# Random-feature attention, a dense layer and a top-1 MoE: the planner gets a shared port and margins, 16 subtractions change from GpSimd to VectorE, the clearing of the output stands later

## The chip, the core and the metric

The kernel runs on one core of a Trainium2 chip. The core has five engines with a queue of instructions each: TensorE (PE, matrix products), VectorE (DVE), ScalarE (ACT), GpSimd (POOL) and SyncE (SP, which here only starts DMA transfers). SBUF and PSUM are the on-chip memories. The metric is the device time in microseconds; lower is better.

## What is computed

```python
# attention with random features; q, k, v: 2 x 8 heads x 576 x 64, omega: 128 x 64
def phi(x):
    h = einsum('bhsd,md->bhsm', x, omega) - sum(x * x, -1) / 2
    return exp(h - max(h, -1)) / sqrt(m)
q_p, k_p = phi(q * scale), phi(k * scale)
kv, z = einsum('bhsm,bhsd->bhmd', k_p, v), sum(k_p, axis=2)
x = einsum('bhsm,bhmd->bhsd', q_p, kv) / (einsum('bhsm,bhm->bhs', q_p, z) + 1e-6)
# dense layer: x 1152 x 512, w_in 512 x 2048, w_out 2048 x 512, both weights as 64-bit floats
h = x @ w_in
y = (h * clip(h + 3, 0, 6) / 6) @ w_out
# MoE: 8 experts, each token to the one with the largest of y @ w_gate, at most 288 tokens each
out[i] = gate[i] * (relu(y[i] @ w1[e]) @ w2[e])      # rows that find no place stay 0
```

## The kernel before

**Attention.** The rows of q and k come in 18 units of 128 x 512, in the order of the list `seq` (five units of k, then q and k alternating, then q). A unit goes through a chain. ScalarE rounds it to its upper half xh (L778); the lower half xl = x - xh is one subtraction of two SBUF tiles (L780), on GpSimd for units 2 to 17 (`X_POOL`), else on VectorE. Then for each of its two halves of 128 x 512 TensorE multiplies with omega (pj, L790), VectorE takes the maximum of each row (nm, L796: 36 of these in all), and ScalarE forms the exponentials (phi, L802), which read the PSUM bank of pj and set it free. Units of k are summed up with v (kvp, L817); those of q are transposed (tpC, L847, copied by ScalarE), multiplied (nd, L863), divided by VectorE (x, L885), transposed again (tpE, L891) and split into the two halves of xT by ScalarE (L914) and VectorE (L917).

**Unpacking the weights.** w_in and w_out come as 16 pieces each of 128 x 512 64-bit numbers, loaded by SyncE (L220, L222) into four buffers. `wlist` gives their order: four pieces of w_in, four of w_out, and so on, 32 in all (weights 0 to 31). Each is turned into 32-bit floats by a chain of five instructions: take the sign off (an AND on VectorE, L248, or, from weight `ABS_FROM` = 12 on, an Abs on ScalarE, L246), clamp (L250), shift (L252), join the lower word (L254), join sign and exponent (L256). A piece of w_in (tiles x, later wsplit) is then split like q and k: the upper half by ScalarE (L262), the lower half by a subtraction (L264, in the plan WL), on GpSimd for weights before `ABS_FROM`, so for eight pieces of w_in, else on VectorE. A piece of w_out (tiles wo) is transposed by TensorE (tpW, L299, in the plan T), copied by ScalarE (woT, L302) and, four at a time, multiplied with the gate's weights (wogp, L309).

**The dense layer.** For each of the 16 f-tiles and each of three groups of 384 tokens there is one block of twelve products hp (L277, 48 blocks); then ScalarE forms t = relu(h + 3) (L281), VectorE g (L285, in the plan Hg), and SyncE writes g to DRAM (L287, L290). The logits of the gate (lg, L334) gather g times the folded gate weights. Then come routing and the experts, which are the same in both kernels but for their place in the queues.

**What sets the order.** Every piece of work is a step of one `Plan`: engine, cost, the steps that it waits for, the buffers that it takes and frees, a rank. `Plan.order` simulates the engines with these costs, always takes the step that could begin first, the lowest rank among those that are ready, and so writes one queue per engine. Rank is a number per kind of step, plus the unit, plus a shift per kind from the table `DELTA`. The chip then runs each queue in just that order; costs and times in the plan have no other effect. A later instruction of a queue never overtakes an earlier one that waits.

The output must hold zeros where no token lands: GpSimd sets a blank tile to 0 (L379) and SyncE writes it nine times over the output (L380), 2304 KB. In the plan this is the step Lout, after `consts`, a string of small GpSimd steps.

Of the kernel before, what the change touches and what calls it, by code (L numbers as in the profile page):

```python
# [39 lines left out]
class Plan:  # L40
# [14 lines left out]
    def add(self, name, engine, cost, emit, after=(), takes=None, frees=(), rank=0.0, early=0.0, then=()):  # L55


        st = dict(
            name=name, engine=engine, cost=cost, emit=emit, after=list(after), frees=list(frees),
            takes=[(takes, name)] if isinstance(takes, str) else takes or [],  # L60
            rank=rank + self.shift, early=early, end=None, then=list(then), kind=self.kind(name),
        )
        self.steps.append(st)
        self.named[name] = st

    def order(self):
# [3 lines left out]
        free_at = {}  # L70
        waiting = {}
# [10 lines left out]
        def begin(st):  # L82
# [17 lines left out]
            return max(free_at[st["engine"]], st["early"], t + self.into.get(st["engine"], 0.0) if t else 0.0)  # L100

        out = []
        for _ in self.steps:
# [15 lines left out]
            free_at[st["engine"]] = st["end"]  # L119
            waiting[st["engine"]].remove(st)  # L120
# [11 lines left out]
def moe_kernel(ctx, tc, q, k, v, v_rest, omega, w_in, w_out, w_gate, w1, w2, out, cap):  # L132
# [31 lines left out]
    X_POOL = set(range(2, 18))  # L164
# [8 lines left out]
    ABS_FROM = 12  # L173
    SLACK = dict(DVE=0.14)
    DELTA = {'consts': 172.4, 'XH0': 7.9, 'XL0': 162.8, 'OM': 17.4, 'OL': -135.3, 'B0': -35.7, 'N0': -102.4, 'P0': 43.4, 'XH1': 5.0, 'XL1': -25.3, 'B1': -28.8, 'N1': -83.0, 'P1': 52.0, 'XH2': 412.1, 'XL2': -95.8, 'B2': -8.2, 'N2': 67.1, 'P2': -3.7, 'KT': 274.4, 'K0': -8.3, 'KW': 141.3, 'KV': -15.6, 'K1': 15.7, 'C1': 127.6, 'T1': 91.1, 'D1': 17.2, 'R1': 27.8, 'S1': -0.4, 'X1': 178.6, 'E1': 182.5, 'EH1': 45.1, 'EL1': -150.5, 'C2': -8.8, 'T2': 158.1, 'D2': 96.9, 'R2': 12.6, 'S2': 129.1, 'X2': 17.9, 'E2': -20.4, 'EH2': 146.6, 'EL2': -87.9, 'KR': -30.3}
# [53 lines left out]

    def w_fetch(key):  # L230
        loaded[key] = w_load(*key)

    def decode(key):
# [30 lines left out]
        (nc.vector if key in abs_act else nc.gpsimd).tensor_tensor(out=t[:, 1, :], in0=xf, in1=t[:, 0, :].bitcast(F32), op=ALU.subtract)  # L264
# [834 lines left out]
    for n, (kd, f) in enumerate(wlist):  # L1099
# [12 lines left out]
        if kd == "i":  # L1112
# [3 lines left out]
                (f"WL{nm}", *(("DVE", 0.6) if (kd, f) in abs_act else ("Pool", 1.25)), dict(after=[f"w{nm}"], frees=[f"W0{nm}"], rank=n if (kd, f) in abs_act else -300)),  # L1116
# [25 lines left out]
    for n, (_, f, g) in enumerate(order):  # L1142
# [5 lines left out]
            (f"Hg{me}", "DVE", 0.47, dict(after=[f"Ht{me}"], takes="g", frees=[f"H{me}", f"Ht{me}"], rank=-500 + n)),  # L1148
# [288 lines left out]
```

## Time and profile before

| | before |
|---|---|
| median of 3 runs | 331.89 us (331.43 to 333.74) |
| profiled execution | 332.73 us |
| its span (first to last instruction) | 330.9 us |
| TensorE clock granted, mean | 0.99 of full speed |
| busy: TensorE, VectorE, ScalarE, GpSimd | 306.9, 222.3, 177.5, 65.4 us |

The busy times are shares of the span of 93, 67, 54 and 20 per cent. Such a share is an average over stages with different limits, so the tables by stage matter more. In the rows further down, x is a tile's name, "x16" a count, and "A <- B" in a table of waits means that A stood until B was done.

### The profile page before, as it was taken

What the parts mean: (1) busy time and instruction counts of PE and PEld (TensorE: products, weight loads), DVE (VectorE), ACT (ScalarE), POOL (GpSimd) and SP (SyncE); (2) the same over time, 40 slices, a digit from 0 to 9 for tenths busy, and PEclk for the clock granted to TensorE, in tenths of its full rate; (3) what the DMA queues carried; (4) which work ended last, traced back from release to release, by engine and by line L of the source; (5) the groups of instructions that cost most, each with busy time, mean ns of one, the idle gap of its engine ahead of it and who ended that gap; (6) DMA issues with size and microseconds to landing.
All of it is one profiled execution on the core that took longest, in us unless ns stands there. A gap on an engine that the chain in (4) does not pass through costs nothing.

```text
span 330.9 us, 6974 instructions
## 1 busy us (share of the span) xinstructions
PE 306.9 (93%) x2570; PEld 278.7 (84%) x2570; DVE 222.3 (67%) x474; ACT 177.5 (54%) x427; POOL 65.4 (20%) x68
## 2 busy tenths in 40 slices
PE   8985989999997798999999999898999999999992
PEld 5884978999987596887989888698999989999781
DVE  5589899999999889889985354749955002764100
ACT  6988799984643545453766324533555132633110
POOL 0774813400240000000000000411513012511021
PEclk9998999999999999999999999999999999999998
DMA  7998662124458777877235127891770004710011
GB/s 245 362 317 309 248 231 66 64 90 137 138 176 254 263 226 234 271 229 223 97 127 184 49 74 244 280 318 57 235 255 1 2 24 101 274 50 0 4 48 32
DMA packets 29675, 54.10 MB, mean 163 GB/s; under 512 B 5536, under 2 KB 18208, under 8 KB 29632
## 3 DMA queue, kind: packets, MB, share of 16 engines
q1 hardware_dynamic: 29248, 52.38, 48.2%
q0 software_dynamic: 384, 1.18, 1.1%
q8 instruction: 22, 0.36, 0.5%
q14 instruction: 21, 0.17, 0.2%
HBM read 37.42 MB, written 16.13 MB: 162 GB/s over the span
## 4 chain that ended last, share of the span: by engine, by line
PE 51%; DVE 15%; DMA 15%; issue 9%; ACT 4%; POOL 2%; SPq 1%; POOLq 0%; ACTq 0%; DVEq 0%
PE hp L277 14%; PE yw L571 14%; PE hp L639 6%; DMA raw<-in_w_in_dram 4%; PE yq L661 4%; PE pj L790 4%; DMA raw<-in_w_out_dram 3%; PE nd L863 3%; DVE nm L796 2%; DMA rawe<-in_w_dram 2%; PE lg L334 2%; DMA out_dram<-scratch,to 2%; DVE g L285 2%; DMA rawx<-in_k_dram 2%; DVE x L252 2%
## 5 line engine op out<-in xcount | busy, mean ns | idle before, releaser
L277 PE MATMUL hp<-xT,wsplit 128*128 128x384 f32 x576 | 107.8, 340 | 0.0
L277 PEld LDWEIGHTS hp<-xT,wsplit 128*128 128x128 f32 x576 | 98.9, 188 | 5.1 <-issue 5.0
L618 POOL TENSOR_TENSOR wsplit<-rawe,wsplit 128x512 fp32r<-128x512 f32 x16 | 22.0, 1379 | 160.6 <-ACT wsplit L616 141.6
L571 PE MATMUL yw<-gh,ohi 128*128 128x288 f32 x256 | 51.9, 298 | 0.2 <-ACT scratch L701 0.2
L281 ACT ACTIVATE t<-hp,three 128x384 f32<-128x384 f32 x48 | 27.6, 578 | 31.4 <-PE hp L277 30.1
L802 ACT ACTIVATE phi<-pj,nm 128x128 f32<-128x128 f32 x144 | 41.0, 414 | 5.5 <-DVE nm L796 5.4
L571 PEld LDWEIGHTS yw<-gh,ohi 128*128 128x128 f32 x256 | 40.8, 188 | 1.3 <-issue 0.6
L285 DVE SCALAR_TENSOR_TENSOR g<-t,hp 128x384 f32<-128x384 f32 x48 | 26.4, 549 | 18.3 <-ACT t L281 17.5
L564 DVE TENSOR_TENSOR gh<-gw,gh 128x288 fp32r<-128x288 f32 x32 | 18.0, 578 | 30.1 <-ACT gh L562 27.8
L571 PE MATMUL yw<-gh,olo 128*128 128x288 f32 x128 | 37.6, 294 | 0.0
L790 PE MATMUL pj<-wbd,xh 128*128 128x256 f32 x144 | 26.3, 305 | 6.5 <-ACT phi L802 5.7
L796 DVE TENSOR_REDUCE nm<-pj 128x4 f32<-128x512 f32 x36 | 24.6, 684 | 5.5 <-ACT phi L802 3.6
L790 PEld LDWEIGHTS pj<-wbd,xh 128*128 128x128 f32 x144 | 19.7, 192 | 10.1 <-ACT phi L802 7.6
L780 POOL TENSOR_TENSOR xl<-rawx,xh 128x512 fp32r<-128x512 f32 x16 | 21.7, 1361 | 30.7 <-ACT xh L778 17.5
L562 ACT ACTIVATE gh<-gw 128x288 fp32r<-128x288 f32 x32 | 14.0, 442 | 23.7 <-PE yw L571 21.1
L639 PE MATMUL hp<-dT,wsplit 128*128 128x288 f32 x192 | 26.3, 296 | 0.4 <-DVE dT L583 0.4
L639 PEld LDWEIGHTS hp<-dT,wsplit 128*128 128x128 f32 x192 | 25.7, 188 | 0.6 <-DVE dT L583 0.6
L571 PEld LDWEIGHTS yw<-gh,olo 128*128 128x128 f32 x128 | 24.1, 189 | 0.0
L616 ACT ACTIVATE wsplit<-rawe 128x512 fp32r<-128x512 f32 x32 | 19.0, 622 | 1.3 <-DMA rawe<-in_w_dram 1.1
L264 POOL TENSOR_TENSOR wsplit<-x,wsplit 128x512 fp32r<-128x512 f32 x8 | 11.6, 1450 | 29.9 <-ACT wsplit L262 29.9
L689 PE MATMUL yp<-wsplit,h 128*96 128x512 f32 (+1 forms) x96 | 16.9, 337 | 0.0
L689 PEld LDWEIGHTS yp<-wsplit,h 128*96 128x96 f32 x96 | 13.5, 162 | 3.4
(147 smaller groups left out, 454.0 us busy)
## 6 DMA issues: line engine op xcount, KB each, us to landing
gall<-g SPq DMA_DIRECT2D x48, 192.0 KB, 3.1
raw<-in_w_in_dram SPq DMA_DIRECT2D x16, 512.0 KB, 4.8
raw<-in_w_out_dram SPq DMA_DIRECT2D x16, 512.0 KB, 4.7
rawe<-in_w_dram SPq DMA_DIRECT2D x16, 512.0 KB, 5.3
gfirst<-g SPq DMA_DIRECT2D x16, 192.0 KB, 3.7
rawx<-in_q_dram SPq DMA_DIRECT2D x9, 256.0 KB, 6.4
out_dram<-blank SPq DMA_DIRECT2D x1, 2304.0 KB, 9.3
gw<-gfirst SPq DMA_DIRECT2D x16, 144.0 KB, 2.6
```

The costliest lines, as they stand in the source:

```text
L277: nc.tensor.matmul(hp, lhsT=w[:, a, wk], rhs=xT[g][b_][:, kk, :], start=(n == 0), stop=(n == 3 * KD - 1))
L281: nc.scalar.activation(out=t, in_=hp, func=ACTF.Relu, bias=three[:, 0:1])
L285: nc.vector.scalar_tensor_tensor(out=gv, in0=t, scalar=6.0, in1=hp, op0=ALU.min, op1=ALU.mult)
L571: nc.tensor.matmul(self.ps[kk], lhsT=wohalf[f][a][:, kk * 128:(kk + 1) * 128], rhs=self.gh[f][:, b_, :], start=(f == YORDER[0] and n == 0) ...
L616: nc.scalar.activation(out=hi, in_=part, func=ACTF.Copy)
L618: engine.tensor_tensor(out=lo, in0=part, in1=hi.bitcast(F32), op=ALU.subtract)
L639: nc.tensor.matmul(hp, lhsT=self.w[0, f][:, a, kk * 128:(kk + 1) * 128], rhs=self.window.dT[b_][:, kk, :], start=(n == 0), stop=(n == 3 * ...
L689: nc.tensor.matmul(ps_, lhsT=self.h2[f // 4, a][:, f % 4, c * SR:(c + 1) * SR], rhs=self.w[1, f][:, b_, x * w:(x + 1) * w], start=(n == 0) ...
L780: (nc.gpsimd if u in X_POOL else nc.vector).tensor_tensor(out=lo[:, sl], in0=rawt[u][:, sl], in1=hi[:, sl].bitcast(F32), op=ALU.subtract)
L790: nc.tensor.matmul(pj[:, 2 * jj:2 * jj + 2, :], lhsT=a[:, j, :], rhs=w, start=(jj == 0 and n == 0), stop=(n == 2), skip_group_check=True,)
L796: nc.vector.tensor_reduce(out=nm, in_=pj, axis=AX.X, op=ALU.max, negate=True)
L802: nc.scalar.activation(out=phis[u][:, 4 * half + h, :], in_=pj[:, h, :], func=ACTF.Exp, bias=nm[:, h:h + 1])
```

## The change

Seven things change.

1. `X_POOL` becomes units 2 to 9: xl of units 10 to 17 is made by VectorE.
2. `POOL_TO = 0`: all lower halves of w_in (WL) are made by VectorE, also those of the first eight pieces.
3. `ABS_FROM` goes from 12 to 8: of weights 8 to 11 the sign is taken off by ScalarE.
4. The plan gets a resource `port`: steps of VectorE and GpSimd whose names match one of two patterns cannot overlap in the plan.
5. The plan gets `lag`: Hg is planned 1.0 us, T 1.5 us behind what they wait for.
6. Lout gets a rank of its own and is planned at 58 us at the earliest; it costs the plan 0.5 and not 6.6 us.
7. Planned costs of the loads are higher, and `DELTA` has new numbers.

The names in the code of steps: W0 to W4 are the five instructions of unpacking, WL the subtraction, XL the subtraction for q and k.

```diff
-            rank=rank + self.shift, early=early, end=None, then=list(then), kind=self.kind(name),
+            port=bool(re.match(r"(XL|WL|v)\d*" if engine == "Pool" else r"(W[0-9L]|XL|OL|ol|gl|v\d)", name)) and engine in ("DVE", "Pool"),
+            rank=rank + self.shift, early=early, lag=lag, end=None, then=list(then), kind=self.kind(name),
...
+        port = [0.0]
...
-            return max(free_at[st["engine"]], st["early"], t + self.into.get(st["engine"], 0.0) if t else 0.0)
+            return max(port[0] if st["port"] else 0.0, free_at[st["engine"]], st["early"], t + self.into.get(st["engine"], 0.0) + st["lag"] if t else 0.0)
...
             free_at[st["engine"]] = st["end"]
+            if st["port"]:
+                port[0] = st["end"]
...
-    X_POOL = set(range(2, 18))
+    X_POOL = set(range(2,10))
...
-    ABS_FROM = 12
+    ABS_FROM = 8
+    POOL_TO = 0
+    LAG_G, LAG_T = 1.0, 1.5
+    OUT_AT = 58.0
...
-    DELTA = {'consts': 172.4, 'XH0': 7.9, 'XL0': 162.8, 'OM': 17.4, 'OL': -135.3, 'B0': -35.7,
...
+    DELTA = {'consts': 116.2, 'XH0': 36.4, 'XL0': 424.6, 'OM': 132.2, 'OL': -14.2, 'B0': 118.9,
...
+    on_pool = set(wlist[:POOL_TO])
...
-        (nc.vector if key in abs_act else nc.gpsimd).tensor_tensor(out=t[:, 1, :], in0=xf, in1=t[:, 0, :].bitcast(F32), op=ALU.subtract)
+        (nc.gpsimd if key in on_pool else nc.vector).tensor_tensor(out=t[:, 1, :], in0=xf, in1=t[:, 0, :].bitcast(F32), op=ALU.subtract)
...
-        load(f"w{i}", lambda: w_fetch(wlist[i]), 1.46, "raww")
+        load(f"w{i}", lambda: w_fetch(wlist[i]), 1.65, "raww")
...
-    load("out", clear_out, 6.6)
-    plan.named["Lout"]["after"].append("consts")
+    plan.add("Lout", "SP", 0.5, clear_out, after=["consts"], rank=-960.0, early=OUT_AT)
...
-                (f"WL{nm}", *(("DVE", 0.6) if (kd, f) in abs_act else ("Pool", 1.25)), dict(after=[f"w{nm}"], frees=[f"W0{nm}"], rank=n if (kd, f) in abs_act else -300)),
+                (f"WL{nm}", *(("Pool", 1.25) if (kd, f) in on_pool else ("DVE", 0.6)), dict(after=[f"w{nm}"], frees=[f"W0{nm}"], rank=-300 if (kd, f) in on_pool else n)),
...
-            (f"Hg{me}", "DVE", 0.47, dict(after=[f"Ht{me}"], takes="g", frees=[f"H{me}", f"Ht{me}"], rank=-500 + n)),
+            (f"Hg{me}", "DVE", 0.47, dict(lag=LAG_G if f < F1T - TAIL else 0.0, after=[f"Ht{me}"], takes="g", frees=[f"H{me}", f"Ht{me}"], rank=-500 + n)),
...
-                (f"T{f}o", "PE", 0.44, dict(after=[f"W4o{f}"] + attended, takes="tp", frees=[f"W0o{f}"], rank=NG * (f - BLOCK) + 0.6)),
+                (f"T{f}o", "PE", 0.44, dict(lag=LAG_T, after=[f"W4o{f}"] + attended, takes="tp", frees=[f"W0o{f}"], rank=NG * (f - BLOCK) + 0.6)),
```

The other loads' costs change likewise (0.73 to 0.83, 1.48 to 1.7). Line numbers of the changed kernel are 8 higher at the loads of the weights (L220 is L228) and 10 higher from there on (L248 is L258).

How the queues look at three places follows; a row has the line, the operation, output tile <- input tiles, and the shape. Names carry a number each, so that rows of one tile can be told.

**VectorE among the row maxima (nm).** The queue from its 17th instruction on, first of the kernel before; x32 is a piece of w_in that is being unpacked:

```order
L248 TENSOR_SCALAR x32_426<-raw_356 128x512
L250 TENSOR_SCALAR x32_426<-x32_426 128x512
L796 TENSOR_REDUCE nm_452<-pj_419 128x4
L252 TENSOR_SCALAR x32_426<-x32_426 128x512
L254 SCALAR_TENSOR_TENSOR x32_426<-raw_356,x32_426 128x512
L256 SCALAR_TENSOR_TENSOR x32_426<-raw_356,x32_426 128x512
L796 TENSOR_REDUCE nm_481<-pj_462 128x4
L248 TENSOR_SCALAR x32_500<-raw_469 128x512
L250 TENSOR_SCALAR x32_500<-x32_500 128x512
L796 TENSOR_REDUCE nm_519<-pj_502 128x4
L252 TENSOR_SCALAR x32_500<-x32_500 128x512
L796 TENSOR_REDUCE nm_541<-pj_522 128x4
```

and of the changed kernel:

```order
L806 TENSOR_REDUCE nm_432<-pj_418 128x4
L258 TENSOR_SCALAR x32_452<-raw_412 128x512
L260 TENSOR_SCALAR x32_452<-x32_452 128x512
L806 TENSOR_REDUCE nm_478<-pj_459 128x4
L806 TENSOR_REDUCE nm_504<-pj_490 128x4
L262 TENSOR_SCALAR x32_452<-x32_452 128x512
L850 TENSOR_TENSOR kvz_530<-kvp_234,kvrs_500 128x8x65
L806 TENSOR_REDUCE nm_543<-pj_519 128x4
L852 TENSOR_TENSOR kvz_530<-kvz_530,kvp_234 128x8
L264 SCALAR_TENSOR_TENSOR x32_452<-raw_412,x32_452 128x512
L806 TENSOR_REDUCE nm_567<-pj_552 128x4
L266 SCALAR_TENSOR_TENSOR x32_452<-raw_412,x32_452 128x512
```

Before, eight unpacking instructions stand among four maxima there; in the changed kernel five stand among five maxima, with two sums of kvz.

**ScalarE where the first transposes of w_out are copied (woT).** Before (t is the ReLU of a hidden block, wsplit the upper half of a piece of w_in, and L246 the Abs of a piece of w_out):

```order
L281 ACTIVATE t_1504<-hp_1472,three_82 128x384
L914 ACTIVATE xT02_98<-tpE_1498 128x2x256
L914 ACTIVATE xT02_98<-tpE_1506 128x2x256
L281 ACTIVATE t_1561<-hp_1513,three_82 128x384
L302 ACTIVATE woT_1569<-tpW_1556 128x512
L302 ACTIVATE woT_1578<-tpW_1563 128x512
L302 ACTIVATE woT_1587<-tpW_1571 128x512
L302 ACTIVATE woT_1603<-tpW_1580 128x512
L262 ACTIVATE wsplit_1608<-x32_1495 128x512
L281 ACTIVATE t_1631<-hp_1589,three_82 128x384
L262 ACTIVATE wsplit_1635<-x32_1585 128x512
L246 ACTIVATE wo_1652<-raw_1605 128x512
```

and of the changed kernel, where L256 is the Abs:

```order
L291 ACTIVATE t_1542<-hp_1485,three_82 128x384
L256 ACTIVATE x32_1546<-raw_1501 128x512
L291 ACTIVATE t_1557<-hp_1529,three_82 128x384
L312 ACTIVATE woT_1574<-tpW_1552 128x512
L291 ACTIVATE t_1588<-hp_1561,three_82 128x384
L312 ACTIVATE woT_1605<-tpW_1583 128x512
L256 ACTIVATE x32_1610<-raw_1577 128x512
L291 ACTIVATE t_1631<-hp_1591,three_82 128x384
L291 ACTIVATE t_1644<-hp_1618,three_82 128x384
L256 ACTIVATE x32_1660<-raw_1615 128x512
L312 ACTIVATE woT_1665<-tpW_1639 128x512
L272 ACTIVATE wsplit_1670<-x32_1546 128x512
```

Before, the first four transposes follow one another behind the first block or two; in the changed kernel they stand one by one between hidden blocks and Abs instructions.

**SyncE around the clearing of the output.** Before (rawx is a unit of q or k, raw a piece of weight, out_0 the output):

```order
L728 DMA rawx_593<-in_q_dram 128x512
L222 DMA raw_600<-in_w_out_dram 128x512
L222 DMA raw_638<-in_w_out_dram 128x512
L380 DMA out_0_dram<-blank_677 128x9x512
L728 DMA rawx_813<-in_q_dram 128x512
L728 DMA rawx_823<-in_q_dram 128x512
L222 DMA raw_839<-in_w_out_dram 128x512
L222 DMA raw_861<-in_w_out_dram 128x512
```

and of the changed kernel, where L390 is the clearing and gall1 and gfirst1 are the first writes of g:

```order
L738 DMA rawx_633<-in_q_dram 128x512
L230 DMA raw_648<-in_w_out_dram 128x512
L738 DMA rawx_681<-in_q_dram 128x512
L738 DMA rawx_744<-in_q_dram 128x512
L230 DMA raw_859<-in_w_out_dram 128x512
L390 DMA out_0_dram<-blank_1146 128x9x512
L230 DMA raw_1152<-in_w_out_dram 128x512
L297 DMA gall1_101<-g_1206 128x384
L300 DMA gfirst1_117<-g_1206 128x384
L230 DMA raw_1353<-in_w_out_dram 128x512
```

Before, the clearing stands ahead of the loads of the last two units of q; in the changed kernel it stands behind them. Six loads of weights stand ahead of it in both, four of them before the first row shown here.

## Rows read from the trace of the kernel before

**Rows 1.** Stages: us, busy time (x instructions) per engine, PEclk, DMA share, GB/s

```profile
16.00:36.00 20.00, 15.60 (x199) 13.82 (x195) 17.22 (x31) 16.92 (x55) 12.60 (x23) 0.91 0.77 270
36.00:54.00 18.00, 16.65 (x222) 15.00 (x220) 17.69 (x37) 15.79 (x49) 7.66 (x6) 1.00 0.71 247
54.00:69.00 15.00, 14.92 (x216) 14.11 (x215) 14.63 (x41) 15.00 (x49) 5.13 (x4) 1.00 0.12 38
...
83.00:101.00 18.00, 16.36 (x128) 14.35 (x127) 17.52 (x28) 9.09 (x18) 5.66 (x4) 1.00 0.54 172
101.00:150.00 49.00, 44.05 (x317) 39.03 (x320) 42.86 (x84) 26.86 (x51) 0.00 (x0) 1.00 0.79 245
150.00:190.00 40.00, 40.00 (x269) 35.12 (x264) 28.72 (x58) 21.07 (x42) 0.00 (x0) 1.00 0.38 133
```

**Rows 2.** Waits, 16 to 75 us: who <- releaser: total us, times, longest

```profile
POOL xl L780 <- ACT xh L778: 9.6, 6, 2.5
...
PE pj L790 <- ACT phi L802: 5.7, 8, 1.9
ACT phi L802 <- DVE nm L796: 5.1, 8, 1.1
```

**Rows 3.** Waits of TensorE, 83 to 174 us, same columns

```profile
PE tpW L299 <- DVE wo L256: 5.3, 4, 2.0
```

**Rows 4.** Timeline of VectorE and GpSimd: start us, us, instruction [idle before]

```profile
93.94 0.42 DVE L250 TENSOR_SCALAR x<-x 128x512 f32<-128x512 f32 x1
94.39 1.38 DVE L252 TENSOR_SCALAR x<-x 128x512 int32<-128x512 int32 x1
...
93.96 1.53 POOL L264 TENSOR_TENSOR wsplit<-x,wsplit 128x512 fp32r<-128x512 f32 x1 [2.47 <-ACT wsplit L262]
```

**Rows 5.** Timeline of VectorE at 102 us, GpSimd idle, same columns

```profile
101.72 0.42 DVE L252 TENSOR_SCALAR wo<-wo 128x512 int32<-128x512 int32 x1
102.17 0.69 DVE L254 SCALAR_TENSOR_TENSOR wo<-raw,wo 128x512 int32<-128x512 int32 x1
102.90 0.69 DVE L256 SCALAR_TENSOR_TENSOR wo<-raw,wo 128x512 int32<-128x512 int32 x1
103.51 0.55 DVE L285 SCALAR_TENSOR_TENSOR g<-t,hp 128x384 f32<-128x384 f32 x1
103.97 0.42 DVE L250 TENSOR_SCALAR wo<-wo 128x512 f32<-128x512 f32 x1
```

**Rows 6.** Groups, whole run, shapes apart: xcount | busy us, mean ns | idle

```profile
L264 POOL TENSOR_TENSOR wsplit<-x,wsplit 128x512 fp32r<-128x512 f32 x8 | 11.6, 1450 | 29.9 <-ACT wsplit L262 29.9
...
L264 DVE TENSOR_TENSOR wsplit<-x,wsplit 128x512 fp32r<-128x512 f32 x8 | 5.5, 687 | 0.1
L246 ACT ACTIVATE x<-raw 128x512 f32<-128x512 f32 x8 | 5.5, 682 | 11.5 <-DMA raw<-in_w_in_dram 10.5 <-DVE wsplit L264 1.1
```

**Rows 7.** Groups of VectorE, 31 to 101 us, same columns

```profile
L256 DVE SCALAR_TENSOR_TENSOR x<-raw,x 128x512 int32<-128x512 int32 x6 | 5.3, 889 | 0.2
L252 DVE TENSOR_SCALAR x<-x 128x512 int32<-128x512 int32 x5 | 5.0, 1004 | 0.2
...
L252 DVE TENSOR_SCALAR wo<-wo 128x512 int32<-128x512 int32 x5 | 3.7, 734 | 0.0
```

**Rows 8.** Chain that ended last, 155 to 180 us: start us, us, what

```profile
158.55 6.26 PE hp L277 x36
164.81 1.42 PE lg L334 x12
...
171.75 2.31 PE hp L277 x12
174.06 0.44 PE tpW L299 x4
```

**Rows 9.** Line L256: min/median/max ns, first to last start

```profile
L256 DVE SCALAR_TENSOR_TENSOR wo<-raw,wo x16: 683/691/958, 49.0 to 163.0; 128x512 int32<-128x512 int32 x16
```

**Rows 10.** Waits of SyncE's queue, whole run, columns of rows 2

```profile
SPq L380 <- POOL blank L379: 6.2, 1, 6.2
```

More of the change, by code (lines that the diff above doesn't have):

```diff
@@ L53, in hold, with add @@
         self.held.append((tag, name))
-    def add(self, name, engine, cost, emit, after=(), takes=None, frees=(), rank=0.0, early=0.0, then=()):
+    def add(self, name, engine, cost, emit, after=(), takes=None, frees=(), rank=0.0, early=0.0, lag=0.0, then=()):
         st = dict(
@@ L172, in moe_kernel @@
     SPLITS = ["PDPDPDPDPDPDPDPD", "PDPDPDPDPDPDPDPD"]
-    ABS_FROM = 12
+    ABS_FROM = 8
+    POOL_TO = 0
+    LAG_G, LAG_T = 1.0, 1.5
+    OUT_AT = 58.0
     SLACK = dict(DVE=0.14)
-    DELTA = {'consts': 172.4, 'XH0': 7.9, 'XL0': 162.8, 'OM': 17.4, 'OL': -135.3, 'B0': -35.7, 'N0': -102.4, 'P0': 43.4, 'XH1': 5.0, 'XL1': -25.3, 'B1': -28.8, 'N1': -83.0, 'P1': 52.0, 'XH2': 412.1, 'XL2': -95.8, 'B2': -8.2, 'N2': 67.1, 'P2': -3.7, 'KT': 274.4, 'K0': -8.3, 'KW': 141.3, 'KV': -15.6, 'K1': 15.7, 'C1': 127.6, 'T1': 91.1, 'D1': 17.2, 'R1': 27.8, 'S1': -0.4, 'X1': 178.6, 'E1': 182.5, 'EH1': 45.1, 'EL1': -150.5, 'C2': -8.8, 'T2': 158.1, 'D2': 96.9, 'R2': 12.6, 'S2': 129.1, 'X2': 17.9, 'E2': -20.4, 'EH2': 146.6, 'EL2': -87.9, 'KR': -30.3}
+    DELTA = {'consts': 116.2, 'XH0': 36.4, 'XL0': 424.6, 'OM': 132.2, 'OL': -14.2, 'B0': 118.9, 'N0': -30.4, 'P0': -58.8, 'XH1': -216.2, 'XL1': 39.7, 'B1': -151.0, 'N1': 36.5, 'P1': 190.2, 'XH2': 114.9, 'XL2': -6.1, 'B2': -56.7, 'N2': -15.1, 'P2': -34.9, 'KT': -190.9, 'K0': 136.8, 'KW': 74.4, 'KV': 235.8, 'K1': 75.1, 'C1': 74.7, 'T1': -65.5, 'D1': -16.0, 'R1': -109.3, 'S1': 65.3, 'X1': -52.2, 'E1': 259.2, 'EH1': -92.3, 'EL1': -150.7, 'C2': -203.3, 'T2': -66.1, 'D2': 70.9, 'R2': 62.4, 'S2': 31.0, 'X2': 149.3, 'E2': -202.5, 'EH2': -212.6, 'EL2': 15.3, 'KR': 23.8}
     RANK = {'A': 0.91, 'B': 1.33, 'C': -3.05, 'D': 2.59, 'E': 3.57, 'EH': 1.06, 'EL': 0.01, 'K': 3.55, 'KV': 3.01, 'N': -2.07, 'P': 2.42, 'R': -1.78, 'T': 3.38, 'XH': -3.59, 'XL': -0.61}
@@ L945, in load_x @@
         for n in range(len(parts)):
-            load(f"x{u}" + "z" * n, lambda: next(gen, None), 0.73 if len(parts) == 1 else 0.47, None if n else "rawx")
+            load(f"x{u}" + "z" * n, lambda: next(gen, None), 0.83 if len(parts) == 1 else 0.47, None if n else "rawx")
     def load_vs(b, c):
-        load(f"v{b}{c}", lambda: load_v(b, c), 1.48, "rawv")
+        load(f"v{b}{c}", lambda: load_v(b, c), 1.7, "rawv")
     load("om", load_omega, 0.47)
@@ L955, in moe_kernel @@
         elif x == "vR":
-            load(x, load_vrest, 1.48)
+            load(x, load_vrest, 1.7)
         elif x[0] == "v":
```

## The prediction, made before the changed kernel ran

> **What bounds the kernel now.** I read the table of stages first [rows 1], because one share for the whole run hides that three stages have three limits. From 16 to 54 us TensorE is busy for 15.60 of 20 and 16.65 of 18 us: it waits, and in the first of the two the granted clock is 0.91. From 54 to 69 us TensorE (14.92), VectorE (14.63) and ScalarE (15.00 of 15) are all full. From 83 to 150 us TensorE waits again (16.36 of 18, 44.05 of 49) while VectorE unpacks 64-bit weights (17.52 of 18). From 150 to 190 us TensorE never stops (40.00 of 40), and from about 180 us on its order of instructions is the same in both kernels. So time can be won or lost only before 150 us, and what is won there reaches the end whole, since all later work follows TensorE.
>
> The waits come second. Up to 75 us TensorE waited 5.7 us in eight places for the exponentials of ScalarE to give a bank back, and ScalarE waited 5.1 us in eight places for the row maximum nm of VectorE [rows 2]. nm is late because it stands in VectorE's queue between unpacking instructions. From 83 us on TensorE waited 5.3 us in four places at a transpose of w_out for VectorE to finish that weight [rows 3]. Altogether 11.0 us of waiting that hangs on VectorE's queue.
>
> The timeline comes third: why is that queue slow? At 93.94 us L250 took 0.42 us. GpSimd began a subtraction of two SBUF tiles at 93.96, and L252 right behind took 1.38 us [rows 4]; the same instruction without GpSimd takes 0.42 [rows 5]. One subtraction on GpSimd (1.53 here, 1.45 in the mean [rows 6]) costs VectorE about 0.95 us when it meets such an instruction, more than the 0.69 us that VectorE needs for the whole subtraction [rows 6]. From 31 to 101 us, where the 16 subtractions lie that now leave GpSimd, the three forms hit hardest lost 5 x (1004 - 420) + 5 x (734 - 420) + 6 x (889 - 690) ns = 5.7 us [rows 7], against 420 and 690 ns when free [rows 5].
>
> **The change, part by part.** *Sixteen subtractions go from GpSimd to VectorE:* xl of units 10 to 17 and the eight w_in pieces that GpSimd still had. One takes 0.687 us [rows 6], of which the next instruction hides some, as L256 with 0.69 us holds the queue for 0.61 [rows 5]: I take 0.65, so +10.4 us of VectorE. Returned: 5.7 us at least, 16 x 0.95 = 15.2 at most. *Four ANDs go to ScalarE* (weights 8 to 11): VectorE is spared 4 x 0.45 = 1.8 us [rows 5]; ScalarE pays 4 x 0.68 [rows 6] behind 83 us, where it is half idle (9.09 of 18 [rows 1]). VectorE's balance is +10.4 - 5.7 - 1.8 = +2.9 us, or with all returned -6.6: about nothing. The Trainium skill (Perfetto Trace Analysis, Optimizing Scalar/DVE Operations) has a rule against it: with a saturated VectorE, giving work to GpSimd may make sense, though its next sentence doubts it between these two, which share a port. By the first half alone the sum would be +10.4 us; the 0.95 us of the row speaks for the second half, and I go by the row.
>
> *When VectorE works changes more.* Before the last nm the old order unpacks seven weights and part of an eighth, the new one four. By the 17th of the 36 maxima the old order holds three whole weights, the new one holds one. Start to start a weight costs 0.45 for L250 and as much for L252, 0.73 for L254 and 0.61 for L256, together 2.24 us [rows 5], so that over attention 3 x 2.24 = 6.7 us and the collisions leave the queue in which nm stands; eight xl (5.2 us) come in, most of them later. What is late next is ScalarE, full from 54 us on [rows 1]. The gain is therefore at most ScalarE's 5.1 us of waits for nm, perhaps an us more for the clock of 0.91, and at least nothing, or a loss if the new order holds nm elsewhere (rivals). Since GpSimd keeps eight xl just there and the new pieces stand in the same queue, I take 4.0.
>
> *After attention* the debt is paid. When the last xT is written, VectorE has finished five weights instead of eight. From there to the eighth transpose of w_out (weight 15) VectorE needs 11 x 2.24 + 4 x 0.65 + 13 x 0.46 (g, L285 [rows 5]) + 2 x 0.45 = 34 us, plus some 1.5 us that it starts later. TensorE now reaches that transpose behind 17 hidden blocks, not 12: three are done at the same place in both orders, so 14 x 2.09, seven transposes x 0.44 and one round of logits of 1.42 [rows 8], with the gate fold 34.5 us; next to other shapes a block takes up to 2.31 [rows 8], so 37 to 38. At the last transpose VectorE has 27 x 2.24 + 12 x 0.65 + 31 x 0.46 = 83 us, + 1.5, and TensorE 32 x 2.09 + 15 x 0.44 and about 6 of logits = 79.5, at 1.09 of it 87 us. The margins are 2 to 3 us and were negative: the four collisions of 87 to 98 us, 4 x 0.95 = 3.8, were about what the first two waits in [rows 3] cost. The old order also had the last weights far ahead: the last L256 at 163.0 us [rows 9], the last transpose at 174.06 [rows 8]; that lead is what is spent. Of the 5.3 us I take 3.5 back (bounds: 0 and 5.3).
>
> *The clearing of the output* moves behind the loads of the last two units. As before six weight loads stand ahead of it, and the sixth needs the buffer of weight 1, which the new order finishes only behind the 22nd maximum. In the old order SP stood 6.2 us at it for GpSimd's memset [rows 10], with the loads of the last two of the 18 units behind it; those are used at the end of attention, so the wait cost nothing and its going gains nothing. The writes should now fall between 54 and 69 us, where the DMA share is 0.12, against 0.71 from 36 to 54 us, where they ran [rows 1]: nothing, at worst one late weight load, 1 to 2 us. *Planned costs, lags and port* change only the order, which is counted above.
>
> Sum: 4.0 + 3.5 = 7.5 us. The profiled execution took 332.73 us (span 330.9 and 1.8 around it), so 325.2; the median of the runs is 0.84 us lower, so **324.5 us**.
>
> **The rivals.** *(a) Forecast:* both halves, 321 to 328, chance 0.52. *(b) Nearly everything:* nm never waits, the clock stays up and no transpose waits, 5.1 + 1 + 5.3 = 11.4 us, about 320.5. For it: three weights fewer stand ahead of nm, and the first waits of [rows 3] come behind six more hidden blocks. Against: weights 8 to 31 have their AND on ScalarE, which also waits there for loads. Chance 0.14. *(c) One half only, or the debt eats the gain:* VectorE's queue is as full as before (17.69 of 18, 14.63 of 15 [rows 1]), the collisions that remain move to other instructions, and the transposes wait as they did; 0 to 4 us, about 330. That is also the case that the plan's port does not hold on the chip. Chance 0.23. *(d) Slower:* a GpSimd that waits for ScalarE's xh holds up nobody; it did so for 9.6 us in six places [rows 2]. On VectorE the same wait holds nm, the attend steps and the unpacking behind it. If all 9.6 us come back there, against the 4.0 and with nothing won later, +5.6 us: 337.5; it decides when VectorE's idle time from 31 to 69 us passes some 4 us (36 to 69 has 0.68 now [rows 1]). Against it: the xl stand behind other work of the same queue, so xh mostly has time. Chance 0.11. The rule of the Trainium skill named above would end on the same side.
>
> The range that leaves out 2 in 10 runs from 319.5 (most of b) to 331.5 (most of c). One per cent, about what a measurement of this kernel can tell, is 3.3 us, so faster means under 328.6: 0.52 + 0.14 and a fifth of c, 0.71; within 1%: 0.18; slower, over 335.2: 0.11.
>
> **What will show it.** VectorE in 36 to 101 us: no L252 or L256 over 1 us with a GpSimd subtraction beside it, except for a few before 35 us. ScalarE's wait for nm up to 75 us: 1 to 2 us instead of 5.1; the last transpose of attention (tpE) near 77 instead of 81 us. TensorE's waits at w_out's transposes: under 2 us. The granted clock near 1.00 throughout. I am wrong in the attention half if nm still ends most waits of ScalarE, and in the second if TensorE stands at transposes for VectorE in the third or fourth group of four, where the margin is the thinnest; a long wait of VectorE for xh would be (d).

## The result, and the profile after

The changed kernel takes 324.01 us (median of 4 runs, 323.43 to 324.44), the kernel before 331.85 us in runs beside it (331.43 to 333.74). The ratio is 0.9752 with a 95% interval of [0.9711, 0.9793]: 7.8 us less. The forecast was 324.5 us in a range of 319.5 to 331.5.

The profiled execution took 323.43 us, its span is 321.7 us at a mean granted clock of 0.99. It lies 0.6 us below its median, and the one of before 0.9 us above its own, so that the two traces differ by 9.2 us where the medians differ by 7.8.

The table by stage of the changed kernel, in the columns and stretches of [rows 1]:

```profile
16.00:36.00 20.00, 17.84 (x254) 15.98 (x252) 15.60 (x31) 19.60 (x66) 8.10 (x21) 1.00 0.80 271
36.00:54.00 18.00, 16.73 (x249) 15.02 (x244) 16.61 (x42) 16.57 (x54) 0.00 (x0) 1.00 0.52 177
54.00:69.00 15.00, 15.00 (x191) 14.32 (x190) 14.14 (x36) 13.75 (x44) 0.00 (x0) 1.00 0.19 63
...
83.00:101.00 18.00, 18.00 (x136) 17.22 (x134) 15.54 (x32) 10.16 (x20) 0.00 (x0) 1.00 0.71 224
101.00:150.00 49.00, 47.82 (x344) 40.85 (x343) 45.79 (x90) 28.06 (x53) 0.00 (x0) 1.00 0.85 265
```

TensorE is busy for 17.84 of 20 us from 16 to 36 us (before 15.60) at the full granted clock (before 0.91), and for 47.82 of 49 from 101 to 150 us (before 44.05). VectorE has room: 15.60 of 20, 16.61 of 18. ScalarE is the full engine from 16 to 36 us now, with 19.60 of 20.

The waits from 16 to 75 us, who <- releaser: total us, times, longest:

```profile
POOL xl L790 <- ACT xh L788: 4.3, 2, 2.8
...
PE pj L800 <- ACT phi L812: 3.3, 6, 0.7
...
ACT phi L812 <- DVE nm L806: 0.5, 2, 0.2
```

ScalarE's wait for the row maxima fell from 5.1 to 0.5 us, TensorE's wait for the exponentials from 5.7 to 3.3 [rows 2]. The waits of TensorE from 83 to 200 us:

```profile
PE wogp L319 <- ACT woT L312: 0.6, 1, 0.6
PE wogt L328 <- ACT wogT L325: 0.6, 1, 0.6
```

No transpose of w_out (tpW, now L309) waits for VectorE any more; before it was 5.3 us [rows 3]. What is left are two waits of 0.6 us at the gate fold. The groups of VectorE from 31 to 101 us, to be held against [rows 7] (L256 is now L266, L252 is L262):

```profile
L266 DVE SCALAR_TENSOR_TENSOR x<-raw,x 128x512 int32<-128x512 int32 x6 | 4.1, 686 | 0.1
...
L262 DVE TENSOR_SCALAR x<-x 128x512 int32<-128x512 int32 x6 | 2.5, 421 | 0.0
...
L262 DVE TENSOR_SCALAR wo<-wo 128x512 int32<-128x512 int32 x4 | 1.7, 424 | 0.1
```

686, 421 and 424 ns, where it was 889, 1004 and 734: they run at their free time. And the line of the last unpacking step of w_out, as in [rows 9]:

```profile
L266 DVE SCALAR_TENSOR_TENSOR wo<-raw,wo x16: 682/691/693, 78.0 to 164.5; 128x512 int32<-128x512 int32 x16
```

The last one starts at 164.5 us and the last transpose at 167.8, a lead of 3.3 us; before it was 163.0 and 174.06, a lead of 11 us [rows 8, 9].

Two places in the traces split the time well: the start of the last group of four transposes of attention (tpE) and the end of the last hidden block (hp). The column "rest" is what is left of the span. The ratio is to runs of the kernel before that were taken beside each kernel; for the experiments their median is 332.00 to 332.55 us.

| kernel | last tpE, us | to the last hp | rest | median, us | ratio to before |
|---|---|---|---|---|---|
| before | 81.5 | 128.2 | 121.3 | 331.85 | |
| after | 78.7 | 122.8 | 120.2 | 324.01 | 0.9752 [0.9711, 0.9793] |
| old_order_vector | 82.3 | 124.6 | 121.2 | 330.64 | 0.9951 [0.9921, 0.9980] |
| new_order_gpsimd | 80.1 | 122.9 | 120.4 | 323.97 | 0.9745 [0.9704, 0.9785] |
| no_lag_t | 79.1 | 122.8 | 120.1 | 323.40 | 0.9731 [0.9697, 0.9766] |
| early_clear | 79.9 | 123.3 | 120.1 | 323.63 | 0.9730 [0.9698, 0.9761] |
| hold_a | 78.2 | 128.8 | 122.1 | 332.65 | 1.0023 [0.9986, 1.0059] |
| late_t4 | 81.3 | 126.1 | 121.4 | 331.45 | 1.0002 [0.9973, 1.0031] |
| no_port | 82.4 | 121.0 | 121.3 | 326.41 | 0.9840 [0.9795, 0.9886] |
| all_vector | 79.6 | 121.2 | 121.1 | 323.50 | 0.9754 [0.9698, 0.9809] |
| hold_booked | 79.9 | 127.3 | 119.5 | 327.90 | 0.9864 [0.9816, 0.9911] |
| booked | 82.3 | 123.4 | 121.3 | 330.22 | 0.9951 [0.9915, 0.9988] |
| hold_vector | 80.4 | 126.2 | 121.7 | 330.27 | 0.9951 [0.9920, 0.9982] |
| xh_first | 78.9 | 123.0 | 121.1 | 323.35 | 0.9734 [0.9696, 0.9772] |

The three parts come from one profiled execution each. Ten runs of hold_a lie between 330.7 and 335.5 us and four of the changed kernel between 323.4 and 324.4, so a difference of an us or two between two traces means little. Medians and ratios rest on 4 to 10 runs of each kernel, against 4 to 23 of the kernel before.

What holds over several traces is the gain in attention. Before, old_order_vector and late_t4, which have the same order there, reach the last tpE at 81.3 to 82.3 us; the six kernels that share the order of the changed one there (xh_first but for two xh) at 78.7 to 80.1; the three with five weights held back at 78.2 to 80.4. That is some 2 us for either way.

### The profile page after: what moved, and what is told of

The parts are those of the page before. It is cut to its first block, busy times and chain, and to the rows that moved or that the text cites. A ratio compares the mean times of both kernels' runs of the same rounds, so it can differ in the third digit from the quotient of the medians.

```text
span 321.7 us, 6957 instructions
## 1 busy us (share of the span) xinstructions
PE 306.2 (95%) x2570; PEld 278.3 (87%) x2570; DVE 217.2 (68%) x486; ACT 179.7 (56%) x431; POOL 42.5 (13%) x52
## 4 chain that ended last, share of the span: by engine, by line
PE 60%; DMA 13%; issue 8%; DVE 8%; ACT 7%; POOL 1%; SPq 1%; POOLq 0%; ACTq 0%; DVEq 0%
PE hp L287 19%; PE yw L581 14%; PE hp L649 7%; PE pj L800 6%; DMA raw<-in_w_out_dram 5%; PE yq L671 4%; DMA raw<-in_w_in_dram 3%; ACT phi L812 2%; PE nd L873 2%; PE lg L344 2%; DMA out_dram<-scratch,to 2%; PE tpC L857 2%; PE kvp L827 2%; DVE g L295 2%; DMA rawx<-in_k_dram 2%
## 5 line engine op out<-in xcount | busy, mean ns | idle before, releaser
L628 POOL TENSOR_TENSOR wsplit<-rawe,wsplit 128x512 fp32r<-128x512 f32 x16 | 22.7, 1421 | 220.4 <-DMA rawe<-in_w_dram 169.9
L574 DVE TENSOR_TENSOR gh<-gw,gh 128x288 fp32r<-128x288 f32 x32 | 16.2, 520 | 29.7 <-ACT gh L572 27.3
L661 DVE SCALAR_TENSOR_TENSOR h<-hp,h 128x288 fp32r<-128x288 f32 x16 | 7.3, 458 | 13.6 <-ACT h L659 13.6
L800 PE MATMUL pj<-wbd,xl 128*128 128x256 f32 x72 | 14.6, 285 | 0.7 <-POOL xl L790 0.6
```

The lines of the kernel that those rows point to most:

```text
L574: nc.vector.tensor_tensor(out=t[:, 1, :], in0=self.raw[f], in1=t[:, 0, :].bitcast(F32), op=ALU.subtract)
L628: engine.tensor_tensor(out=lo, in0=part, in1=hi.bitcast(F32), op=ALU.subtract)
L800: nc.tensor.matmul(pj[:, 2 * jj:2 * jj + 2, :], lhsT=a[:, j, :], rhs=w, start=(jj == 0 and n == 0), stop=(n == 2), skip_group_check=True,)
```

## The experiments

### The engine apart from the order

The plan sets the order, and the instruction's engine is chosen where it is issued. So the two can be taken apart: the order of one kernel with the engines of the other.

**old_order_vector**: the order of before, the 16 subtractions on VectorE.

```diff
-            (nc.gpsimd if u in X_POOL else nc.vector).tensor_tensor(out=lo[:, sl], ...
+            (nc.gpsimd if u in range(2, 10) else nc.vector).tensor_tensor(out=lo[:, sl], ...
-        (nc.vector if key in abs_act else nc.gpsimd).tensor_tensor(out=t[:, 1, :], ...
+        nc.vector.tensor_tensor(out=t[:, 1, :], ...
```

> The order of the kernel before, unchanged; only the engine of the 16 subtractions (xl of units 10 to 17, eight pieces of w_in) is VectorE when they are issued. Theory M (the lock costs the time: VectorE is held by GpSimd's subtractions): most of the 7.8 us come back without any new order, 325 to 327 us, and the waits at w_out's transposes fall from 5.3 to under 2.5 us, since the four collisions just ahead of them (3.8 us) are gone. Theory O (the order earns it: fewer weights among the maxima, transposes later): 331 to 333 us, as VectorE's account of this move alone is about nothing (16 x 0.65 given, 11 taken back), ScalarE's wait for nm stays near 5 us. My prediction had both in it: 328 to 330.

Measured: 330.64 us, 1.6 us less by the ratio. Its waits from 16 to 75 us:

```profile
ACT phi L802 <- DVE nm L796: 7.0, 11, 1.4
PE pj L790 <- ACT phi L802: 5.5, 6, 1.9
```

and TensorE's at the transposes from 83 us on:

```profile
PE tpW L299 <- DVE wo L256: 2.6, 2, 1.8
```

Behind attention the collisions were worth something in the old order: 2.6 us of waits instead of 5.3, and 124.6 us to the last hp instead of 128.2. In attention ScalarE waits longer for nm than before, 7.0 us against 5.1; eight more subtractions now stand in VectorE's queue. The move alone earns a fifth of the result; theory M is out, theory O's 331 is missed by a little.

**new_order_gpsimd**: the order of the changed kernel, the same 16 subtractions on GpSimd.

```diff
-            (nc.gpsimd if u in X_POOL else nc.vector).tensor_tensor(out=lo[:, sl], ...
+            (nc.gpsimd if u in range(2, 18) else nc.vector).tensor_tensor(out=lo[:, sl], ...
-        (nc.gpsimd if key in on_pool else nc.vector).tensor_tensor(out=t[:, 1, :], ...
+        (nc.gpsimd if key in wlist[:12] else nc.vector).tensor_tensor(out=t[:, 1, :], ...
```

> The order of the changed kernel, unchanged; only the engine of the same 16 subtractions is GpSimd when they are issued. Theory M: the collisions are back (16 of some 0.95 us, though VectorE is spared 16 x 0.65), 329 to 332 us, with L262 or L266 over 1 us beside GpSimd's work. Theory O: 323 to 325 us, as after. The prediction's mixture: 326 to 328, the loss mainly behind 80 us, where the eight pieces of w_in are split.

Measured: 323.97 us, the time of the changed kernel. The collisions are back; VectorE's timeline at 100 us (start us, us, instruction), and GpSimd's beside it:

```profile
100.81 1.69 DVE L264 SCALAR_TENSOR_TENSOR x<-raw,x 128x512 int32<-128x512 int32 x1
102.54 1.65 DVE L266 SCALAR_TENSOR_TENSOR x<-raw,x 128x512 int32<-128x512 int32 x1
...
105.03 1.75 DVE L264 SCALAR_TENSOR_TENSOR wo<-raw,wo 128x512 int32<-128x512 int32 x1
```

```profile
100.67 2.98 POOL L274 TENSOR_TENSOR wsplit<-x,wsplit 128x512 fp32r<-128x512 f32 x2 [5.02 <-ACT wsplit L272]
104.94 1.29 POOL L274 TENSOR_TENSOR wsplit<-x,wsplit 128x512 fp32r<-128x512 f32 x1 [1.29 <-ACT wsplit L272]
```

Three instructions of 0.69 us take 1.65 to 1.75. Yet no transpose waits; from 83 to 200 us TensorE waits only here:

```profile
PE wogp L319 <- ACT woT L312: 1.3, 2, 0.7
```

VectorE loses about 1 us in a collision and is spared 0.69 us of its own work: in an order that has 0.6 us of VectorE booked for each of these subtractions, that is nearly the same. The time is theory O's; a difference under some 1.3 us the runs could not tell.

**all_vector**: the order of the changed kernel, and also xl of units 2 to 9 on VectorE.

```diff
-            (nc.gpsimd if u in X_POOL else nc.vector).tensor_tensor(out=lo[:, sl], ...
+            nc.vector.tensor_tensor(out=lo[:, sl], ...
```

> The changed kernel's order, unchanged, but xl of units 2 to 9 is issued on VectorE as well, so that GpSimd makes no lower halves of rows at all. VectorE gets 8 x 0.65 = 5.2 us more between 12 and 30 us, where it was busy 15.6 of 20 us. Theory 'the engine of a subtraction does not matter while the queue has room': 323 to 325.5 us. Rival 'GpSimd's eight still earn something': nm waits behind them, ScalarE's wait for nm passes 2 us, 326 to 329.

Measured: 323.50 us, no difference. What GpSimd keeps in the changed kernel is worth nothing either way.

### The margin at the transposes and the place of the clearing

**no_lag_t**

```diff
-    LAG_G, LAG_T = 1.0, 1.5
+    LAG_G, LAG_T = 1.0, 0.0
```

> The changed kernel without the margin of 1.5 us at the transposes (LAG_T = 0); the order up to the end of attention is the same, the transposes stand one hidden block earlier at most places (T0 behind 4, not 5, T4 behind 14, not 15). Theory 'margin': the waits of TensorE at tpW for VectorE come back at three or four transposes, 1 to 3 us, 325 to 327. Rival 'slack': the six blocks that T4 moved come from the rest of the plan, one block of 2.1 us is not needed, no wait over 0.5 us, 323.5 to 324.5.

Measured: 323.40 us. The wait that comes back is small:

```profile
PE tpW L309 <- DVE wo L266: 1.2, 3, 0.6
```

1.2 us in three places, which the median does not show. The margin LAG_T is not what earns; one hidden block more or less at T is covered.

**early_clear**

```diff
     steps = plan.order()
+    names = [st["name"] for st in steps]
+    steps.insert(names.index("Lx16"), steps.pop(names.index("Lout")))
```

> The changed kernel with the clearing of the output issued ahead of the load of the 17th unit, where it stood before. As predicted (its place is worth nothing): 323.5 to 324.5, SyncE waits some us for the blank tile and the last two units land later but in time. Rival (the writes of 2304 KB and SyncE's wait hold up loads that are needed): xh of the last two units or the third w_out piece waits for its DMA, 1 to 3 us more.

Measured: 323.63 us. The writes are issued at 30.4 us instead of 42.1 and take 11.0 us to land in both; the wait for the blank tile that I expected of SyncE did not come. The place of the clearing is worth nothing.

### What in the order earns: two parts taken into the old plan

**hold_a**: the kernel before, with earliest times for the unpacking of five weights.

```diff
+    HELD = {0: 22.0, 1: 35.0, 2: 50.0, 3: 62.0, 4: 74.0}
...
         chain(decode((kd, f)), steps)
+        if n in HELD:
+            plan.named[f"W0{nm}"]["early"] = HELD[n]
```

> The kernel before with one thing added: in the plan the first five weights may not begin to be unpacked before 22, 35, 50, 62 and 74 us of planned time. Engines, table, costs, clearing and everything else as before; the GpSimd subtractions stay on GpSimd. In the order the first four weights are then done behind the 14th, 22nd, 33rd and 36th maximum (before: 11, 14, 17, 20; changed kernel: 15, 22, 30, 35), and without any margin the transposes T0, T4, T8, T12 move to 5, 14, 24, 32 hidden blocks (before 4, 9, 18, 27; changed 5, 15, 23, 32). Theory 'held back' (the late unpacking is what the new order earns by): 323 to 327 us. Rival 'table' (the new table of ranks and the new costs do it): 329 to 333 us. Rival 'lock': the collisions just ahead of the transposes stay, 328 to 330.

Measured: 332.65 us, no gain, so my theory fell in this form. Up to the last tpE it does all that the changed kernel does: 78.2 us against 81.5. Behind it TensorE still stands for VectorE and ScalarE, now at later blocks:

```profile
PE tpW L300 <- DVE wo L257: 4.1, 4, 2.8
PE lg L335 <- ACT wog L322: 1.1, 1, 1.1
PE wogp L310 <- ACT woT L303: 0.6, 1, 0.6
```

4.1 us at the transposes, 5.8 with the logits and the gate fold; before it was 5.3 at the transposes and 1.2 at the gate fold. So this trace shows waits that stay, not waits that grow, and 1.8 us of the 3.3 are left at its end. But the profiled execution was the better case, 1.7 us under the median, and by the medians nothing is left. That what attention won is a loan from VectorE, which the transposes collect, is my reading; where the slower executions lose it, no trace shows.

**late_t4**: the kernel before, with a margin at T only (the rest of its edit gives the old plan the field `lag`).

```diff
-                (f"T{f}o", "PE", 0.44, dict(after=...
+                (f"T{f}o", "PE", 0.44, dict(lag=4.0, after=...
```

> The kernel before with one thing added: a margin of 4 us at the transposes of w_out. The order up to the end of attention is the same; T0 stands behind 6 blocks instead of 4, T4 behind 12 instead of 9, T8 behind 19 instead of 18. Theory 'held back': it is only the second half of the gain, the waits at tpW (5.3 us in the profile of before) fall to 0 to 2 us and 327 to 329 us result, with the attention half as before. Rival 'moved wait': TensorE then waits for VectorE elsewhere (a hidden block whose w_in piece is late), 330 to 333 us.

Measured: 331.45 us, no difference. No transpose waits any more, but TensorE now waits one step on, at the gate fold and the logits:

```profile
PE wogp L309 <- ACT woT L302: 3.0, 3, 1.3
PE lg L334 <- ACT wog L321: 1.2, 1, 1.2
```

That is the rival's "moved wait", in another place than I had named. The transposes went only part of the way here: T4, T8 and T12 stand behind 12, 19 and 28 blocks, in the changed kernel behind 15, 23 and 32.

**no_port**: the changed kernel, the port not booked.

```diff
-            if st["port"]:
-                port[0] = st["end"]
```

> The changed kernel with the port switched off in the plan; all else as changed. The order then finishes the first weights behind 12, 15, 22 and 31 maxima (changed: 15, 22, 30, 35) and T4 stands behind 13 blocks (15). Theory 'held back': it lies between the two kernels, 325 to 328 us. Rival 'the port is only a disturbance of the order': 323 to 325, no difference that can be measured.

Measured: 326.41 us, 0.984 instead of 0.975. As expected it lies between, and the trace has the loss in attention (last tpE 82.4 us; from there to the last hp it is 1.8 us faster than the changed kernel, behind it 1.1 slower); the waits from 16 to 75 us (line numbers are two lower here):

```profile
PE pj L798 <- ACT phi L810: 5.9, 8, 1.2
...
ACT phi L810 <- DVE nm L804: 3.3, 4, 2.0
```

In the changed kernel they are 3.3 and 0.5. So the port earns 2 to 3 us, though the collisions that it models cost nothing in the new order (new_order_gpsimd). What it changes in the order is that the first weights are done later, behind 15, 22, 30 and 35 maxima and not 12, 15, 22 and 31.

### The account

In the old plan the subtraction of a piece of w_in is 1.25 us of GpSimd and nothing of VectorE. The next three kernels ask what it is worth to book it.

**hold_booked**: hold_a, the eight lower halves booked on VectorE, still issued on GpSimd.

```diff
-                (f"WL{nm}", *(("DVE", 0.6) if (kd, f) in abs_act else ("Pool", 1.25)), dict(... rank=n if (kd, f) in abs_act else -300)),
+                (f"WL{nm}", "DVE", 0.6, dict(... rank=n)),
```

> As hold_a (the kernel before, five weights held back), and the plan now also books the eight lower halves of w_in as 0.6 us of VectorE each; on the chip they still run on GpSimd, as do all xl of units 2 to 17. Table, costs and clearing as before. The transposes T4, T8, T12 move to 16, 25, 34 blocks (hold_a 14, 24, 32). hold_a won 3.3 us up to the last tpE and lost it at tpW (4.1 us of waits). Theory 'account' (the plan has to book on VectorE what a GpSimd subtraction costs VectorE there): the waits at tpW fall under 1.5 us, 325 to 328 us. Rival 'lock' (a collision of 1 us just ahead of a transpose is paid whatever the plan books): 330 to 333 us.

Measured: 327.90 us, within what theory 'account' expected, with every subtraction on the engine it had before, the old table and the old clearing. TensorE's waits at the transposes:

```profile
PE tpW L300 <- ACT x L247: 2.3, 1, 2.3
PE tpW L300 <- DVE wo L257: 0.9, 1, 0.9
```

VectorE ends 0.9 us of them, not 4.1. The other wait is a new one, and ScalarE's timeline shows where it is from (in brackets the idle time ahead, and what ended it):

```profile
147.64 0.68 ACT L247 ACTIVATE x<-raw 128x512 f32<-128x512 f32 x1 [4.66 <-DMA raw<-in_w_in_dram]
148.23 0.56 ACT L282 ACTIVATE t<-hp,three 128x384 f32<-128x384 f32 x1
148.69 0.58 ACT L303 ACTIVATE woT<-tpW 128x512 f32<-128x512 f32 x1
```

An Abs (L247) stood 4.66 us for a load, and the copies of two transposed weights (woT) stood behind it.

TensorE's busy time from 101 to 150 us, first here, then in hold_a:

```profile
101.00:150.00 49.00, 46.54 (x311) 39.78 (x309) 41.78 (x78) 24.48 (x46) 3.88 (x3) 1.00 0.74 239
```

```profile
101.00:150.00 49.00, 44.17 (x307) 37.02 (x311) 44.21 (x82) 24.99 (x46) 2.61 (x3) 1.00 0.78 245
```

It stands 2.5 us there, in hold_a 4.8. Yet the trace does not place the gain that the medians give. The experts' first product (yw) begins at the same time in both, after the same work of TensorE, here and in hold_a:

```profile
209.29 0.53 PE L572 MATMUL yw<-gh,ohi 128*128 128x288 f32 x2
```

```profile
209.31 0.53 PE L572 MATMUL yw<-gh,ohi 128*128 128x288 f32 x2
```

The whole 2.3 us by which this span is shorter lies behind, where the order came out another way too and the routing's wait of 1.0 us is gone. This execution also lost the full clock twice:

```profile
16.00:36.00 20.00, 16.33 (x209) 15.02 (x210) 11.49 (x23) 16.55 (x56) 11.04 (x23) 0.91 0.88 310
150.00:190.00 40.00, 38.23 (x272) 33.65 (x272) 37.36 (x68) 26.35 (x53) 0.00 (x0) 0.96 0.52 175
```

The granted clock (the column before the DMA share) is 0.91 in the first stretch and 0.96 in the second, behind the wait for the load; in hold_a's it is 1.00 in both. Whether that hid a lead at 209 us, no run shows. That the two changes together win 4.5 us rests on the medians alone.

**booked**: the booking alone, nothing held back (the same edit in the kernel before).

> The kernel before with the eight lower halves of w_in booked as VectorE time in the plan, and nothing held back; on the chip they stay on GpSimd. Weights done behind 11, 14, 17, 22, 28 and 32 maxima (before 11, 14, 17, 20, 24, 30), T4, T8, T12 behind 10, 19, 28 blocks (before 9, 18, 27). Theory 'account': attention as before, waits at tpW 2 to 4 us instead of 5.3, 328 to 331 us. Rival 'lock': 331 to 333.

Measured: 330.22 us. The waits at the transposes are down to 1.3 us, less than I expected; attention is as before:

```profile
PE tpW L299 <- DVE wo L256: 1.3, 3, 0.7
```

**hold_vector**: the order of hold_a, the eight lower halves issued on VectorE and not booked there (the second edit of old_order_vector).

> The order of hold_a, unchanged; only the engine of the eight lower halves of w_in is VectorE when they are issued. Theory 'lock': the collisions behind 90 us are gone and with them most of the 4.1 us at tpW, 326 to 328.5 us. Theory 'account': VectorE now needs 8 x 0.65 us that the order did not reckon with, about as much as the collisions took, so the waits stay at 2.5 to 5 us and the time at 330 to 333.

Measured: 330.27 us, and waits of

```profile
PE tpW L300 <- DVE wo L257: 1.9, 3, 1.2
PE wogp L310 <- ACT woT L303: 1.5, 1, 1.5
```

The time is within theory 'account', the waits at tpW lie below its 2.5 us: taking the collisions away earns 0.7% on hold_a, booking them earns 1.6%.

### An attempt to gain more

**xh_first**

```diff
     steps = plan.order()
+    for mv, at in [('XH2', 'P01'), ('XH3', 'P01')]:
+        names = [st["name"] for st in steps]
+        steps.insert(names.index(at), steps.pop(names.index(mv)))
```

> The changed kernel, but ScalarE makes xh of units 2 and 3 ahead of the eight exponentials of unit 1, as the kernel before did (there xh of the third unit began at 8.4 us, in the changed kernel at 10.2). If the late start costs: the fifth maximum comes at 11 and not at 13 us, and 1 to 2 us of it reach the end, 322 to 323.3 us. If ScalarE sets the pace from 16 to 36 us in the changed kernel (19.6 of 20 us busy), which it must work off in any order: 323.5 to 324.5.

Measured: 323.35 us, no difference from the changed kernel. xh of the third unit began at 8.2 us, but the fifth maximum still came at 13.0. TensorE's timeline shows why: the new order sums up both first units (kvp) ahead of the next pj, and the second sum waits for the exponentials that xh now delays.

```profile
7.62 1.16 PE L827 MATMUL kvp<-rawv,phi 128*64 128x65 f32 x32
9.84 2.15 PE L827 MATMUL kvp<-rawv,phi 128*64 128x65 f32 x32 [1.07 <-ACT phi L812]
11.92 0.73 PE L800 MATMUL pj<-wbd,xh 128*128 128x256 f32 x4
```

## Why the prediction was right, step by step

**The sum.** From the two traces 2.8 us were won up to the last tpE (forecast 4.0), 5.3 from there to the last hp (forecast 3.5), and 1.1 behind it (forecast 0): 9.2 against 7.5, and 7.8 by the medians. The sizes of the two halves were off in opposite directions, so that the sum came out as near as it did is in part luck. (7.5 off 332.73 and then 0.84 is 324.4, not 324.5.) A part of it goes with the clock: the mean granted clock is 0.973 to 0.997 in 23 runs of before and 0.994 to 0.997 in four of the changed kernel. The two runs of before with 0.996 and 0.997 took 330.7 and 330.6 us, so by an estimate from these two some 6.6 of the 7.8 us are left at an equal clock.

**VectorE's account, "about nothing": shown in the new order.** It was the step that spoke against a common reading of this change, that taking work off GpSimd is the gain. The order of the changed kernel takes 323.97 us with the 16 subtractions on GpSimd and 324.01 without. In the old order, which had no room booked for these subtractions, the move earns 1.6 us.

**Attention.** The mechanism, fewer weights unpacked ahead of nm, is shown by hold_a: five times in the old plan bring the last tpE to 78.2 us. It is not the clock of 0.91 from 16 to 36 us: booked has 1.00 there and its last tpE at 82.3. ScalarE's wait for nm fell further than I said (0.5 us, not 1 to 2). That the gain is smaller than 4.0 I put down to the next limit: ScalarE is full from 16 to 36 us, and the new order starts worse, with the fifth maximum at 12.9 us against 11.0. xh_first shows that an earlier xh alone does not mend this start; the sums of kvp stand ahead in TensorE's queue.

**"What is won there reaches the end whole"** held in the traces to about an us. From one instruction on (176.4 us before, 168.2 after) TensorE's order is the same to the end: the changed kernel is 8.2 us ahead there and 9.2 at the end, hold_a 2.9 and 1.8. What the sentence does not cover is the way from attention to that point: that the attention half and the dense half add up was taken for granted. hold_a won 3.3 us in attention, and its median is not below that of before.

**The dense layer.** I reckoned margins of 2 to 3 us at the eighth and the last transpose, thin but positive, and took 3.5 of 5.3 back. All 5.3 came back. Two other waits fell by 0.6 us each, at the gate fold (wogt) and at the logits, to 0.6 and 0.5; before they were

```profile
PE wogt L318 <- ACT wogT L315: 1.2, 1, 1.2
PE lg L334 <- DVE g L285: 1.1, 1, 1.1
```

and 0.6 us at wogp is new. What I called the spent lead is seen: 3.3 us at the last transpose instead of 11. I put the gain down to where the transposes stand. late_t4, which moves them part of the way, gives nothing, and no_lag_t shows that the margin is not needed. What tells, as far as the runs go, is that the order reckons with VectorE's time. Two changes of the old plan, held-back unpacking and the booking, earn nothing and 1.6 us alone and 4.5 together, on the old engines. That the booking works by keeping VectorE's room behind attention fits the transposes (VectorE's share of the waits is 4.1 us in hold_a, 0.9 in hold_booked), but it is argued: hold_booked also moves the transposes up to two blocks further and changes the order behind the last hp, and where its time is won the trace does not show.

**The rule of the Trainium skill** that I weighed (Perfetto Trace Analysis, Optimizing Scalar/DVE Operations: with a saturated VectorE, work may go to GpSimd) would by its first half have cost 10.4 us here, by my estimate. The run new_order_gpsimd agrees with its doubt instead: in the new order these 16 subtractions cost the same time on either engine.

**The clearing** was priced rightly and placed wrongly: it was issued at 42.1 us, not between 54 and 69.

**The rivals.** Of (c), that the waits only move: in the changed kernel they did not, in late_t4 they did, and in hold_a they stayed, at later blocks. That the port does not hold on the chip is half true: as a lock it isn't needed, as an item in the plan it earns 2 to 3 us. VectorE's wait for xh (d) did not appear from 31 to 101 us. One wait of the same kind did, for the upper half of a piece of w_in, without TensorE standing for it:

```profile
DVE wsplit L274 <- ACT wsplit L272: 2.1, 1, 2.1
```


**Open.** From hold_booked (327.9) to the changed kernel 3.9 us are left for the new table, the port, the higher costs of loads, the margin at Hg, the four ANDs and the bookings of xl together; of these only the port was taken out by itself. The wait for a load in hold_booked points to the costs of the loads. The reverse test, the changed plan without the booking of the subtractions on VectorE, was not made either, so how much of its 7.8 us the booking earns is not known.

## What to carry to other kernels

When a planner writes the order, a wrong entry in its account can cost more than the thing that it leaves out: in the new order which engine did the work made no difference, while in the old plan booking it and holding other work back won 4.5 us, over half as much as the whole change. Take the two apart before you explain such a change, by issuing the same order on the other engine. And a gain in one stage that comes from putting work off may be a loan: hold_a's 3.3 us in attention show in no median. Look in the next stage for what it costs, and compare medians, not two traces.

## What the hardware showed that I had not expected

Not every instruction of VectorE is held by a subtraction on GpSimd. In the thirteen traces with some of them among the maxima (all but all_vector), 127 row maxima began while one ran, and each took 0.67 to 0.69 us; the unpacking instructions took up to 1.8. In the changed kernel two subtractions ran from 18.68 us on (2.74 us); a row maximum, which reads PSUM, took its 0.69 us beside them, a clamp in SBUF 1.39:

```profile
19.25 0.69 DVE L806 TENSOR_REDUCE nm<-pj 128x4 f32<-128x512 f32 x1 [1.94 <-ACT phi L812]
...
20.31 1.39 DVE L260 TENSOR_SCALAR x<-x 128x512 f32<-128x512 f32 x1
```

```profile
18.68 2.74 POOL L790 TENSOR_TENSOR xl<-rawx,xh 128x512 fp32r<-128x512 f32 x2
```

The Trainium skill (SBUF — State Buffer, Who interferes with whom) says that an instruction of VectorE with at most one input in SBUF, outside the modes that use both ports, does not contend with GpSimd. The maxima agree with it. The clamp reads one tile in SBUF and was lengthened; whether it ran in such a mode no run shows. So GpSimd's subtractions were harmless beside maxima and lengthened the unpacking.
